# A condition for overfull experts, moved from between two stages to behind the last store

## The chip, the cores and the metric

The kernel runs on one core of a Trainium2 chip. The metric is device time of one execution in microseconds (us). The core has five engines that run side by side, each with an instruction queue of its own, and meet only through semaphores: TensorE (PE, with its weight loads shown apart as PEld), VectorE (DVE), ScalarE (ACT), GpSimd (POOL) and SyncE (SP), which issues most DMA transfers here. POOL issues the indirect ones, in which every row goes to an address of its own. A conditional jump is an instruction of an engine's sequencer. All five engines have to take the same decision, so each has its own copy of it.

## The reference

Three layers follow each other. The first is an attention in which a query sees only the keys whose six hash bits equal its own (2 batches, 8 heads, 768 positions, head size 64). Its output is 1536 tokens of 512 numbers. The second is a mixture of experts: each token goes to the one of 8 experts with the largest gate value.

```
e_idx = np.argmax(x @ w_gate, axis=1)
for e in range(E):
    mask = e_idx == e
    h = np.maximum(x[mask] @ w1[e], 0.0)
    out[mask] = gate_w[mask, None] * eom[mask, e, None] * (h @ w2[e])
```

The third is a feed-forward layer with a gated softmax (`solu = h * softmax(h)`), a normalization over 1024 channels, and a product with `w_out`.

```
h = x @ w_in
solu = h * softmax(h)
ln = (solu - mean(solu)) / sqrt(var(solu) + 1e-6) * g_ln
out = ln @ w_out
```

How many tokens an expert gets is known only on the chip. The draw used here gives the experts 192, 202, 210, 177, 218, 182, 193 and 162 tokens.

## The kernel before, in words

Every engine's instructions stand in the order in which the code writes them; there is no scheduler behind it. The Tile layer adds the semaphore waits.

The attention fills the first 250 us. It scatters each token's row, grouped by expert, to a table `xs` in memory, and counts the tokens of each expert. From the counts `totals` sorts the experts and works out where each one's columns start. It also computes a number `win[:, 3]`: how many extra passes ("windows" of `WIN = 160` tokens) are needed because an expert has more tokens than its capacity (`CAPS`: 224, 224, 224, 212, 200, 192, 184, 168 in sorted order, the first two being experts 0 and 1). For the counts above it is 0.

The expert stage runs 64 slots: four groups of `mm1` (L1167 to L1169) or `mm2` (L1196 to L1198) each. Every product is taken with fp16 high and low parts, so it has three matmuls. `ev2` evicts a result of `mm2` into `yT`, the transposed token columns: the high part by ACT (L1205), the low part by DVE (L1206, put off by one group through `run_late`). A column group of an expert starts at a position that is read from a register.

Behind the last slot stands `overflow()` (L1306; L1126 and L1127 are in it). Each engine loads `win[:, 3]` into a register and jumps over the body if it is 0. The body holds a loop over the extra windows with a full `mm1` and `mm2`.

The last stage (L1308 on) has 12 tiles of 128 tokens. `h2(t)` is 24 matmuls of 512 columns on PE (L1323) into a PSUM buffer of two banks, of which there are three. `solu_a` to `solu_d` are done by DVE, ACT and, for a power, POOL. The result is transposed by a DMA. `outp(t)` is 24 matmuls of 512 columns (L1391) and follows `h2(t + 4)` on PE. ACT evicts each output tile (L1395). For the last tile ACT takes the first 256 columns and DVE the other 256 (L1397). POOL copies the tile's row numbers to `tok` (L1399) and stores the tile with an indirect DMA (L1401). At the end of the program each engine drains, and all five meet at a barrier; those instructions carry L1452.

Some weights of the last stage (`w_in`, `w_out`) arrive as 64-bit floats. They are decoded piece by piece in free places of ACT (L125), POOL (L130, L152) and DVE (L135, L141, L146, L171).

Of the kernel before, what the change touches and what calls it, by code (L numbers as in the profile page):

```python
# [21 lines left out]
def kernel(  # L22
# [988 lines left out]
    with tc.manual_schedule():  # L1011
# [78 lines left out]

        wt["wo", 0] = yp.tile([128, 2, 4096], F16, name="wo")
        yT = yp.tile([128, 2, KD, NT + CAP], F16, name="yT")
        xw_t, hh_t = {}, {}

        def x_load(e, r0, w=CAP):
            xw = mp.tile([128, 2 * KD, CAP], F16, tag="xw", name="xw", bufs=3)
            x = nc.sync.dma_start_transpose(out=xw[:, :, 0:w], in_=xs[r0, :])
            xw_t[e] = xw
            if e in (1, "x"):
                for y in scattered:  # L1100
                    tc.add_manual_dep(x.ins, y.name, mybir.DependencyInfo(
                        mybir.DependencyClass.Sync, mybir.DependencyReason.DATA), reason="rows of xs")

        def window():

            d = nc.vector
            nf, sf, done = (exp_f[:, x] for x in range(3))
            f, win_f = (mp.tile([1, x, y], F32, tag=nm, name=nm, bufs=1) for x, y, nm in ((8, E, "wf"), (1, 3, "wg")))
            m = mp.tile([1, 1], F32, tag="wm", name="wm", bufs=1)
            d.tensor_tensor(out=f[:, 0], in0=nf, in1=done, op=ALU.is_gt)  # L1110
            d.scalar_tensor_tensor(out=f[:, 0], in0=iota8[0:1], scalar=1.0, in1=f[:, 0], op0=ALU.add, op1=ALU.mult)
            d.tensor_reduce(out=m, in_=f[:, 0], op=ALU.max, axis=AX.X)
            d.tensor_tensor(out=f[:, 0], in0=f[:, 0], in1=m.to_broadcast([1, E]), op=ALU.is_equal)
            d.tensor_scalar(out=f[:, 1], in0=nf, scalar1=-float(WIN), scalar2=None, op0=ALU.add)
            d.tensor_tensor(out=f[:, 1], in0=f[:, 1], in1=done, op=ALU.min)
            d.tensor_tensor(out=f[:, 2], in0=f[:, 1], in1=row0[0:1], op=ALU.add)
            d.tensor_tensor(out=f[:, 3], in0=f[:, 1], in1=sf, op=ALU.add)
            d.tensor_copy(out=f[:, 4], in_=iota8[0:1])
            d.tensor_tensor(out=f[:, 5:8], in0=f[:, 2:5], in1=f[:, 0:1].to_broadcast([1, 3, E]), op=ALU.mult)
            d.tensor_reduce(out=win_f[:, 0], in_=f[:, 5:8], op=ALU.add, axis=AX.X)  # L1120
            d.tensor_copy(out=win[:, 0:3], in_=win_f[:, 0])
            d.scalar_tensor_tensor(out=done, in0=f[:, 0], scalar=float(WIN), in1=done, op0=ALU.mult, op1=ALU.add)

        def overflow():
            why = "made on the chip from token counts"
            n = nc.values_load(win[:, 3:4], min_val=0, max_val=MW, skip_runtime_bounds_check_because=why)  # L1126
            with tc.If(n != 0), tc.For_i(0, n, 1) as i:  # L1127
                window()
                r0, c0, e0 = (
                    nc.values_load(win[0:1, x:x + 1], engines=g, min_val=0, max_val=mx,  # L1130
                                   skip_runtime_bounds_check_because=why)
                    for x, g, mx in ((0, [ET.SP], E * NT - WIN), (1, [ET.DVE, ET.Activation], NT), (2, [ET.SP], E - 1)))
                x_load("x", bass.ds(r0, WIN), WIN)
                for name, src, tag in (("w1", w1, "wa"), ("w2", w2, "wb")):
                    t16 = wp.tile([128, 2, 4096], F16, tag=tag, name=tag)
                    for c in range(4):
                        t = raw.tile([128, 1024], F32, tag="raw", name="raw")
                        if name == "w1":
                            nc.sync.dma_start(out=t, in_=src[bass.ds(e0, 1), c * 128:(c + 1) * 128, :]
                                              .rearrange("e p f -> (e p) f"))  # L1140
                        else:
                            nc.sync.dma_start(out=t.rearrange("p (f d) -> p f d", f=2),
                                              in_=src[bass.ds(e0, 1), c * 256:(c + 1) * 256, :]
                                              .rearrange("e (f p) d -> p (e f) d", p=128))
                        cs = slice(c * 1024, (c + 1) * 1024)
                        nc.scalar.activation(out=t16[:, 0, cs], in_=t, func=AF.Copy, scale=W_S)
                        nc.vector.scalar_tensor_tensor(out=t16[:, 1, cs], in0=t, scalar=W_S, in1=t16[:, 0, cs],
                                                       op0=ALU.mult, op1=ALU.subtract)
                    wt[name, "x"] = t16
                for g in range(4):  # L1150
                    ev1("x", g, mm1("x", g, WIN), WIN)
                    run_late()
                for g in range(4):
                    mm2("x", g, WIN)
                    ev2("x", g, c0, WIN)
                    run_late()
# [25 lines left out]
        def run_late():  # L1182
            for f in late:
                f()
            late.clear()
# [117 lines left out]
                nc.vector.tensor_scalar(out=csc, in0=mr[:, :, 0], scalar1=float(2.0 ** -22), scalar2=None,  # L1303
                                        op0=ALU.mult)
        run_late()
        overflow()  # L1306

        moe.close()  # L1308
        ps_a = ctx.enter_context(tc.tile_pool(name="ps_a", bufs=2, space=PSUM, reuse_waits="tile"))
        ps_h = ctx.enter_context(tc.tile_pool(name="ps_h", bufs=3, space=PSUM, reuse_waits="tile"))  # L1310
        mp = ctx.enter_context(tc.tile_pool(name="mq", bufs=2, reuse_waits="tile"))
# [73 lines left out]

        def outp(t):
            zT, fr = zT_t.pop(t), fr_t.pop(t)
            ps = ps_a.tile([128, DM], F32, tag="a", name="o")
            for f in range(KF):
                for a, w in ((0, 0), (0, 1), (1, 0)):  # L1390
                    nc.tensor.matmul(ps, zT[:, KF * a + f], w_o[:, w, f], start=(f == 0 and a == 0 and w == 0),  # L1391
                                     stop=(f == KF - 1 and a == 1))
            o = mp.tile([128, DM], F32, tag="o", name="o", bufs=3)
            na = DM if t < NTILE - 1 else DM // 2
            nc.scalar.activation(out=o[:, 0:na], in_=ps[:, 0:na], func=AF.Copy, scale=fr)  # L1395
            if na < DM:
                nc.vector.tensor_scalar(out=o[:, na:], in0=ps[:, na:], scalar1=fr, scalar2=None, op0=ALU.mult)  # L1397
            to = tok[:, t:t + 1]
            nc.gpsimd.tensor_scalar(out=to, in0=slot_f[:, t:t + 1], scalar1=1.0, scalar2=1.0, op0=ALU.mult,  # L1399
                                    op1=ALU.mult)  # L1400
            x = nc.gpsimd.indirect_dma_start(  # L1401
                out=out[:, :], out_offset=bass.IndirectOffsetOnAxis(ap=to, axis=0),
                in_=o, in_offset=None).ins
            for y in stored:
                tc.declare_no_dep(x, y, reason="every token has a row of its own")
            stored.append(x)
# [16 lines left out]
                outp(t - LAG)  # L1423
        for t in range(NTILE - 1 - LAG, NTILE):
            outp(t)


# [29 lines left out]
```

## Time and profile before

| | us |
|---|---|
| median of 3 runs | 526.81 (526.65 to 527.11) |
| profiled execution, its own time | 526.2 |
| its span, from the first to the last instruction | 524.4 |
| PE busy | 501.5 (96%) |
| DVE busy | 389.5 (74%) |
| ACT busy | 317.4 (61%) |
| POOL busy | 283.2 (54%) |

The profile is one execution. Its own time is 1.8 us above its span. All positions below are microseconds from the start of the span. A busy time says how long an engine had something in work. What an engine waited for stands in square brackets behind the instruction that ended the wait, or in the view of one source line. A letter q behind an engine (PEldq, POOLq, SPq) is its sequencer, where loads of registers, jumps, waits for semaphores and drains run. [...]

### The profile page before, as it was taken

The page shows a single profiled execution, that of the slowest core. Times are in us where ns is not written, and L with a number is a line of the kernel's source. Part 1 is how long each engine was busy: PE and PEld are TensorE (multiplying, and loading weights), DVE is VectorE, ACT ScalarE, POOL GpSimd, SP SyncE. Part 2 cuts the span into 40 slices and gives each one's busy share as a digit, 9 for nine tenths or more (in the row PEclk, how much of TensorE's full clock was granted, in tenths as well). Part 3 has the DMA queues.
Part 4 walks back from the last instruction along what each step waited for, and adds up shares of the span by engine and source line. Part 5 has one row for each costly group of instructions (what it writes and reads, how often), then busy time and mean ns, then how long its engine had stood idle before and what let it go on. Part 6 is the DMA issues. An engine that isn't in the chain of part 4 may idle for free. (4 is left out here: it accounts for less than half of the span.)

```text
span 524.4 us, 12447 instructions
## 1 busy us (share of the span) xinstructions
PE 501.5 (96%) x4692; PEld 384.7 (73%) x4692; DVE 389.5 (74%) x926; ACT 317.4 (61%) x595; POOL 283.2 (54%) x433
## 2 busy tenths in 40 slices
PE   7799999999999999997999999999979999999994
PEld 4578787888787888886999999999854444444442
DVE  7788888888888888766489898969934887455610
ACT  5778787888778887881364665566612455334420
POOL 7999896969879796826166587212111012212131
PEclk9999999999999999998999999999999999999998
DMA  5678988763837675302699999998500236352250
GB/s 180 144 201 188 243 151 236 194 184 86 201 115 126 200 174 167 78 2 81 194 288 227 314 307 296 272 313 279 173 5 0 55 76 112 80 96 66 61 140 40
DMA packets 107183, 83.23 MB, mean 159 GB/s; under 512 B 80624, under 2 KB 89456, under 8 KB 107120
## 3 DMA queue, kind: packets, MB, share of 16 engines
q1 hardware_dynamic: 104816, 76.09, 57.8%
q0 software_dynamic: 2304, 6.31, 3.1%
q8 instruction: 38, 0.62, 0.5%
q14 instruction: 25, 0.20, 0.1%
HBM read 51.43 MB, written 9.97 MB: 117 GB/s over the span
## 5 line engine op out<-in xcount | busy, mean ns | idle before, releaser
L627 PE MATMUL t<-ident,p 128*128 128x128 f32 x576 | 126.1, 275 | 0.5
L615 ACT ACTIVATE p<-s,mx 128x768 f32<-128x768 f32 x96 | 95.7, 997 | 38.7 <-DVE mx L604 22.4
L600 DVE TENSOR_REDUCE mx<-s 128x1 f32<-128x768 f32 x96 | 91.6, 955 | 27.0 <-PE s L590 21.6
L629 ACT COPY pt<-t 128x384 f32<-128x384 f32 x192 | 85.5, 479 | 7.0 <-PE t L627 5.8
L627 PEld LDWEIGHTS t<-ident,p 128*128 128x128 f32 x576 | 77.8, 141 | 15.4 <-ACT pt L629 8.9
L651 PE MATMUL v<-pt,v 128*64 128x128 f32 x1128 | 72.0, 277 | 0.0
L1323 PE MATMUL h<-wi,yT 128*128 128x512 f16 x288 | 65.2, 386 | 2.9 <-PEq L1127 2.9
L651 PEld LDWEIGHTS v<-pt,v 128*64 128x64 f32 x1128 | 60.6, 137 | 7.8 <-issue 6.8
L1197 PE MATMUL a<-hh,wb 128*128 128x224 f16 (+5 forms) x256 | 63.4, 251 | 2.0 <-DVE hh L1176 1.9
L1391 PE MATMUL o<-wo,zT 128*128 128x512 f16 x288 | 63.6, 379 | 0.1
L130 POOL TENSOR_SCALAR dm<-dm 128x512 f32<-128x512 f32 x16 | 33.2, 2072 | 56.4 <-ACT dm L125 56.2
L1196 PE MATMUL a<-hh,wb 128*128 128x224 f16 (+5 forms) x256 | 63.4, 251 | 0.0
L1198 PE MATMUL a<-hh,wb 128*128 128x224 f16 (+5 forms) x256 | 63.4, 251 | 0.0
L590 PE MATMUL s<-k,q 128*128 128x384 f16 x192 | 59.0, 329 | 1.0 <-ACT p L615 1.0
L590 PE MATMUL s<-b,cm 128*128 128x384 f16 x192 | 57.2, 326 | 1.4 <-DVE b L552 1.4
L1323 PEld LDWEIGHTS <-yT 128*128 128x128 f16 x288 | 28.6, 99 | 38.0 <-issue 5.4
L1167 PE MATMUL a<-xw,wa 128*128 128x224 f16 (+5 forms) x224 | 55.2, 249 | 0.3 <-DVE hh L1176 0.3
L1169 PE MATMUL a<-xw,wa 128*128 128x224 f16 (+5 forms) x224 | 55.2, 249 | 0.0
L1168 PE MATMUL a<-xw,wa 128*128 128x224 f16 (+5 forms) x224 | 55.2, 249 | 0.0
L1391 PEld LDWEIGHTS <-zT 128*128 128x128 f16 x288 | 28.2, 98 | 34.3 <-issue 0.4
L1401 POOL DMA_INDIRECT out_dram<-o,tok x12 | 12.6, 1047 | 53.8 <-issue 46.9
L1339 ACT ACTIVATE ex<-h,st,csc 128x1024 f32<-128x1024 f32 x12 | 14.4, 1203 | 41.8 <-DVE st L1362 27.6
(269 smaller groups left out, 1031.4 us busy)
## 6 DMA issues: line engine op xcount, KB each, us to landing
raw<-in_moe_w_dram SPq DMA_DIRECT2D x64, 512.0 KB, 6.1
raww<-in_moe_w_in_dram SPq DMA_DIRECT2D x8, 512.0 KB
raww<-in_moe_w_out_dram SPq DMA_DIRECT2D x8, 512.0 KB
xs<-raw SPq DMA_DIRECT2D x8, 448.0 KB, 4.0
v<-in_v_dram SPq DMA_DIRECT2D x8, 384.0 KB
q<-in_q_dram SPq DMA_DIRECT2D x6, 384.0 KB
k<-in_k_dram SPq DMA_DIRECT2D x6, 384.0 KB, 5.6
cm<-q SPq DMA_DIRECT2D x14, 96.0 KB, 2.1
```

The lines of the kernel that those rows point to most:

```text
L590: nc.tensor.matmul(t[:, c, 0:SB], d[x, h][:, s], flat(d[y, h])[:, c * SB:(c + 1) * SB], start=first, stop=not first)
L600: nc.vector.tensor_reduce(out=mx[:, 0:1], in_=t[:, :, 0:SB], op=ALU.max, axis=AX.XY)
L615: nc.scalar.activation(out=p, in_=s_t.pop(i)[:, :, 0:SB], func=AF.Exp, scale=mx[:, 1:2], bias=mx[:, 2:3], accum_out=sums[j][:, qt, h:h + 1])
L627: nc.tensor.transpose(t[:, g * 128:(g + 1) * 128], p[:, c, g * 128:(g + 1) * 128], ident)
L629: nc.scalar.copy(out=pt[i][:, 3 * c:3 * c + 3], in_=t[:, 0:SB].rearrange("p (g c) -> p g c", g=3))
L651: nc.tensor.matmul(o[64 * h:64 * h + 64], vt[:, h, c], ph[h][:, c], start=(c == 0), stop=(c == NS - 1), tile_position=(0, 64 * h))
L1167: nc.tensor.matmul(ps[:, i, 0:n], w[:, 0, kk, fs], xw[:, kk], start=(kk == 0), stop=False)
L1196: nc.tensor.matmul(ps, w[:, 0, f, ds], hh[:, 0, f], start=(f == 0), stop=False)
L1197: nc.tensor.matmul(ps, w[:, 0, f, ds], hh[:, 1, f], start=False, stop=False)
L1198: nc.tensor.matmul(ps, w[:, 1, f, ds], hh[:, 0, f], start=False, stop=(f == KF - 1))
L1323: nc.tensor.matmul(ps[:, c], yT[:, a, kk, ts], w_i[:, w, kk, c * 512:(c + 1) * 512], start=(kk == 0 and a == 0 and w == 0), stop=(kk == KD ...
L1391: nc.tensor.matmul(ps, zT[:, KF * a + f], w_o[:, w, f], start=(f == 0 and a == 0 and w == 0), stop=(f == KF - 1 and a == 1))
```

## The change

Four edits belong together.

1. `window()` and `overflow()` move behind the last `outp`. Nothing stands any more between the last slot of the expert stage and the last stage.
2. Since the last stage has then run without the extra tokens, the body of the condition runs the whole last stage once more after its loop. With a count of 0 the body is jumped over as before.
3. `yT` is set to zero before the expert stage, since columns of tokens over the capacity would otherwise be read before they are written.
4. The last output tile is computed in two halves of 256 columns, each with a PSUM buffer and 24 matmuls of its own, and both halves are evicted by ACT.

```
         yT = yp.tile([128, 2, KD, NT + CAP], F16, name="yT")
+        nc.gpsimd.memset(yT.bitcast(F32)[:, :, :, 0:NT // 2], 0.0)
...
         run_late()
-        overflow()
 
         moe.close()
...
         def outp(t):
             zT, fr = zT_t.pop(t), fr_t.pop(t)
-            ps = ps_a.tile([128, DM], F32, tag="a", name="o")
-            for f in range(KF):
-                for a, w in ((0, 0), (0, 1), (1, 0)):
-                    nc.tensor.matmul(ps, zT[:, KF * a + f], w_o[:, w, f], start=(f == 0 and a == 0 and w == 0),
-                                     stop=(f == KF - 1 and a == 1))
             o = mp.tile([128, DM], F32, tag="o", name="o", bufs=3)
             na = DM if t < NTILE - 1 else DM // 2
-            nc.scalar.activation(out=o[:, 0:na], in_=ps[:, 0:na], func=AF.Copy, scale=fr)
-            if na < DM:
-                nc.vector.tensor_scalar(out=o[:, na:], in0=ps[:, na:], scalar1=fr, scalar2=None, op0=ALU.mult)
+            for c0 in range(0, DM, na):
+                cs = slice(c0, c0 + na)
+                ps = ps_a.tile([128, DM], F32, tag="a", name="o")[:, 0:na]
+                for f in range(KF):
+                    for a, w in ((0, 0), (0, 1), (1, 0)):
+                        nc.tensor.matmul(ps, zT[:, KF * a + f], w_o[:, w, f, cs], start=(f == 0 and a == 0 and w == 0),
+                                         stop=(f == KF - 1 and a == 1))
+                nc.scalar.activation(out=o[:, cs], in_=ps, func=AF.Copy, scale=fr)
...
         for t in range(NTILE - 1 - LAG, NTILE):
             outp(t)
 
+        last.close()
+        stored.clear()
+        mp = ctx.enter_context(tc.tile_pool(name="mo", bufs=1, reuse_waits="tile"))
...
+        def overflow():
+            why = "made on the chip from token counts"
+            n = nc.values_load(win[:, 3:4], min_val=0, max_val=MW, skip_runtime_bounds_check_because=why)
+            with tc.If(n != 0):
+                with tc.For_i(0, n, 1):
+                    window()
...
+                for t in range(NTILE):
+                    solu_a(t, h2(t))
+                    solu_b(t)
+                    solu_c(t)
+                    solu_d(t)
+                    outp(t)
+
+        overflow()
```

In the order of the instructions the change shows at three places. The first is PE between the two stages. Before, the last `mm2` is followed by the load of the count, the jump, and the body of the condition:

```order
L1198 LDWEIGHTS wb
L1198 MATMUL a<-hh,wb 128x168
L1126 TENSOR_LOAD win [waits DVE_49]
L1127 COMPARE_AND_BRANCH x2
L1127 UNCONDITIONAL_BRANCH [waits PE_49]
L1127 UNCONDITIONAL_BRANCH [waits barrier_Pool_Activation_PE_DVE_SP_release]
L1452 BRANCH_PREFETCH_HINT
```

After the change `h2(0)` (now L1270) stands directly behind the last `mm2` (now L1145), with waits for the three engines that write what it reads:

```order
L1145 LDWEIGHTS wb
L1145 MATMUL a<-hh,wb 128x168
L1270 LDWEIGHTS yT [waits Activation_49,Pool_49]
L1270 MATMUL h<-wi,yT 128x512 [waits DVE_49]
L1270 LDWEIGHTS yT
L1270 MATMUL h<-wi,yT 128x512
```

The load and the jump are gone from here, and so are the rows of the body: on PE there are 385 rows from the `TENSOR_LOAD` to the first matmul weights of the last stage before. At the end of the program the jump now leads over some 1,590 rows on PE, 206 on DVE, 74 on ACT and 44 on POOL.

The second place is the end of ACT's queue, with the last output tiles. Before, one eviction of 256 columns ends it, and DVE does the other half:

```order
L1395 ACTIVATE o<-o,fr 128x512 [waits DMASW6_49,PE_49,Activation_49]
L1395 ACTIVATE o<-o,fr 128x512 [waits DMASW7_49,PE_49,Activation_49]
L1395 ACTIVATE o<-o,fr 128x256 [waits DVE_49,DMASW0_49,PE_49,Activation_49]
L1452 UNCONDITIONAL_BRANCH
```

Now ACT has both halves (L1344), and the load and the jump follow:

```order
L1344 ACTIVATE o<-o,fr 128x512 [waits DMASW7_49,PE_49,Activation_49]
L1344 ACTIVATE o<-o,fr 128x256 [waits DVE_49,DMASW0_49,PE_49,Activation_49]
L1344 ACTIVATE o<-o,fr 128x256 [waits PE_49]
L1400 TENSOR_LOAD win [waits DVE_49]
L1401 COMPARE_AND_BRANCH
```

The second half waits for PE alone. The third place is the end of POOL's queue. Before, the last store is followed by the end of the program:

```order
L1399 TENSOR_SCALAR tok<-slot_f 128x1
L1401 DMA out_dram<-o,tok 1536x512 [waits DMASW2_49,Activation_49,Pool_49]
L1399 TENSOR_SCALAR tok<-slot_f 128x1
L1401 DMA out_dram<-o,tok 1536x512 [waits DMASW3_49,DVE_49,Pool_49]
L1452 UNCONDITIONAL_BRANCH
L1452 ISA [waits barrier_Pool_Activation_PE_DVE_SP_gather]
```

After the change the path that jumps over the body ends the queue. It stands in the last three rows here; the two rows ahead of them are the end of the body, a store of the repeated stage:

```order
L1346 TENSOR_SCALAR tok<-slot_f 128x1
L1348 DMA out_dram<-o,tok 1536x512 [waits DMASW7_49,Activation_49,Pool_49]
L1401 UNCONDITIONAL_BRANCH
L1401 ISA [waits Pool_49,DMASW4_49,DMASW5_49,DMASW3_49,DMASW6_49,DMASW2_49,DMASW7_49,DMASW1_49,DMASW0_49]
L1401 UNCONDITIONAL_BRANCH
L1466 ISA [waits barrier_Pool_Activation_PE_DVE_SP_gather]
```

On this path POOL waits until all its stores have landed (DMASW0 to DMASW7), and then adds to their semaphores what the stores of the skipped body would have added (the `ISA` row of L1401). SP, which waits for these semaphores at the end of the program, goes on only then.

## Rows read from the trace of the kernel before

**Rows 1.** First part of the page: busy us (share of the span) xinstructions.

```profile
PE 501.5 (96%) x4692; PEld 384.7 (73%) x4692; DVE 389.5 (74%) x926; ACT 317.4 (61%) x595; POOL 283.2 (54%) x433
```

**Rows 2.** By stretch: length; PE, PEld, DVE, ACT, POOL busy; granted clock; DMA share, GB/s.

```profile
388.20:391.00 2.80, 0.00 (x0) 0.02 (x1) 0.51 (x1) 1.08 (x2) 1.08 (x1) 1.00 0.04 12
391.00:400.00 9.00, 8.99 (x34) 3.76 (x35) 2.50 (x4) 0.34 (x1) 0.84 (x1) 0.81 0.01 2
400.00:450.00 50.00, 50.00 (x233) 22.70 (x232) 36.95 (x99) 25.41 (x37) 8.67 (x13) 1.00 0.40 76
```

**Rows 3.** Timeline between the stages: start, us, instruction, [idle before, its releaser].

```profile
387.90 0.24 PE L1198 MATMUL a<-hh,wb 128*128 128x168 f16 x1
388.17 0.45 ACT L1205 ACTIVATE yT<-a 128x336 f32 x1 [3.03 <-PE a L1198]
388.65 0.51 DVE L1206 SCALAR_TENSOR_TENSOR yT<-a,yT 128x336 f32 x1 [2.97 <-ACT yT L1205]
391.01 2.60 PE L1323 MATMUL h<-wi,yT 128*128 128x512 f16 x7 [2.88 <-PEq L1127]
398.08 1.22 DVE L1336 TENSOR_REDUCE st<-h 128x1 f32<-128x1024 f32 x1 [5.05 <-PE h L1323]
```

**Rows 4.** L1126 and L1127 by sequencer: ns min/median/max, first and last start.

```profile
L1126 PEldq TENSOR_LOAD <-win x1: 486/486/486, 386.7 to 386.7; - x1
L1127 PEldq COMPARE_BRANCH  x1: 3423/3423/3423, 387.3 to 387.3; - x1
L1127 POOLq COMPARE_BRANCH  x1: 45/45/45, 374.7 to 374.7; - x1
```

**Rows 5.** Other gaps of PE, and the granted clock around them.

```profile
382.39 0.23 PE L1197 MATMUL a<-hh,wb 128*128 128x168 f16 x1 [0.95 <-DVE hh L1176]
380.00:384.00 4.00, 2.95 (x40) 2.67 (x38) 3.23 (x6) 0.32 (x1) 0.00 (x0) 1.00 0.02 4
240.00:244.00 4.00, 1.20 (x16) 0.94 (x17) 3.37 (x28) 0.30 (x1) 2.63 (x6) 1.00 0.18 70
244.00:248.00 4.00, 4.00 (x28) 3.41 (x26) 1.60 (x14) 0.00 (x0) 3.04 (x7) 0.60 0.34 138
392.00:394.00 2.00, 2.00 (x6) 0.76 (x5) 1.00 (x2) 0.00 (x0) 0.00 (x0) 0.50 0.00 0
```

**Rows 6.** Timeline of the last output tile, and one stretch of small matmuls.

```profile
517.56 0.47 ACT L1395 ACTIVATE o<-o,fr 128x256 f32<-128x256 f32 x1 [4.49 <-PE o L1391]
518.07 0.48 DVE L1397 TENSOR_SCALAR o<-o,fr 128x256 f32<-128x256 f32 x1 [15.38 <-ACT o L1395]
519.32 1.00 POOL L1401 DMA_INDIRECT out_dram<-o,tok  x1 [4.25 <-issue]
386.00:388.00 2.00, 2.00 (x30) 1.92 (x27) 0.00 (x0) 0.00 (x0) 0.00 (x0) 1.00 0.00 0
```

**Rows 7.** L1452 at the end of the program, by sequencer; and a small POOL instruction.

```profile
L1452 SPq EVENT_SEMAPHORE  x1: 17658/17658/17658, 504.4 to 504.4; - x1
L1452 SPq DRAIN  x2: 7/10/13, 522.6 to 522.7; - x2
L1452 POOLq DRAIN  x1: 4447/4447/4447, 519.1 to 519.1; - x1
514.88 0.19 POOL L1399 TENSOR_SCALAR tok<-slot_f 128x1 int32<-128x1 f32 x1
```

**Rows 8.** A memset, and POOL, DVE and PE at the start of the expert stage.

```profile
L305 POOL MEMSET raw<- x1: 942/942/942, 33.6 to 33.6; 128x1024 f32 x1
261.46 1.93 POOL L130 TENSOR_SCALAR dm<-dm 128x512 f32<-128x512 f32 x1 [11.05 <-ACT dm L125]
258.41 0.28 DVE L846 RECIPROCAL me<-rz 128x3 f32<-128x3 f32 x3
269.23 0.26 PE L1196 MATMUL a<-hh,wb 128*128 128x224 f16 x1
269.71 0.61 DVE L1176 SCALAR_TENSOR_TENSOR hh<-a,hh 128x448 f16<-128x448 f32 x1
```

More of the change, by code (lines that the diff above doesn't have):

```diff
@@ L1092 @@
         yT = yp.tile([128, 2, KD, NT + CAP], F16, name="yT")
+        nc.gpsimd.memset(yT.bitcast(F32)[:, :, :, 0:NT // 2], 0.0)
         xw_t, hh_t = {}, {}
         def x_load(e, r0, w=CAP):
-            xw = mp.tile([128, 2 * KD, CAP], F16, tag="xw", name="xw", bufs=3)
+            xw = mp.tile([128, 2 * KD, CAP], F16, tag="xw", name="xw", bufs=1 if e == "x" else 3)
             x = nc.sync.dma_start_transpose(out=xw[:, :, 0:w], in_=xs[r0, :])
@@ L1102, in x_load @@
                         mybir.DependencyClass.Sync, mybir.DependencyReason.DATA), reason="rows of xs")
[L1104 to L1156, printed above, removed]
@@ L1310 @@
         ps_h = ctx.enter_context(tc.tile_pool(name="ps_h", bufs=3, space=PSUM, reuse_waits="tile"))
-        mp = ctx.enter_context(tc.tile_pool(name="mq", bufs=2, reuse_waits="tile"))
+        last = ExitStack()
+        mp = last.enter_context(tc.tile_pool(name="mq", bufs=2, reuse_waits="tile"))
         w_i = wt["wi", 0].rearrange("p a (k f) -> p a k f", k=KD)
@@ L1425, with window @@
             outp(t)
+        last.close()
+        stored.clear()
+        mp = ctx.enter_context(tc.tile_pool(name="mo", bufs=1, reuse_waits="tile"))
+        def window():
+            d = nc.vector
+            nf, sf, done = (exp_f[:, x] for x in range(3))
+            f, win_f = (mp.tile([1, x, y], F32, tag=nm, name=nm, bufs=1) for x, y, nm in ((8, E, "wf"), (1, 3, "wg")))
+            m = mp.tile([1, 1], F32, tag="wm", name="wm", bufs=1)
+            d.tensor_tensor(out=f[:, 0], in0=nf, in1=done, op=ALU.is_gt)
+            d.scalar_tensor_tensor(out=f[:, 0], in0=iota8[0:1], scalar=1.0, in1=f[:, 0], op0=ALU.add, op1=ALU.mult)
+            d.tensor_reduce(out=m, in_=f[:, 0], op=ALU.max, axis=AX.X)
+            d.tensor_tensor(out=f[:, 0], in0=f[:, 0], in1=m.to_broadcast([1, E]), op=ALU.is_equal)
+            d.tensor_scalar(out=f[:, 1], in0=nf, scalar1=-float(WIN), scalar2=None, op0=ALU.add)
+            d.tensor_tensor(out=f[:, 1], in0=f[:, 1], in1=done, op=ALU.min)
+            d.tensor_tensor(out=f[:, 2], in0=f[:, 1], in1=row0[0:1], op=ALU.add)
+            d.tensor_tensor(out=f[:, 3], in0=f[:, 1], in1=sf, op=ALU.add)
+            d.tensor_copy(out=f[:, 4], in_=iota8[0:1])
+            d.tensor_tensor(out=f[:, 5:8], in0=f[:, 2:5], in1=f[:, 0:1].to_broadcast([1, 3, E]), op=ALU.mult)
+            d.tensor_reduce(out=win_f[:, 0], in_=f[:, 5:8], op=ALU.add, axis=AX.X)
+            d.tensor_copy(out=win[:, 0:3], in_=win_f[:, 0])
+            d.scalar_tensor_tensor(out=done, in0=f[:, 0], scalar=float(WIN), in1=done, op0=ALU.mult, op1=ALU.add)
@@ new lines, in overflow @@
+        def overflow():
[4 more added lines that the diff above has]
+                    window()
+                    r0, c0, e0 = (
+                        nc.values_load(win[0:1, x:x + 1], engines=g, min_val=0, max_val=mx,
+                                       skip_runtime_bounds_check_because=why)
+                        for x, g, mx in ((0, [ET.SP], E * NT - WIN), (1, [ET.DVE, ET.Activation], NT), (2, [ET.SP], E - 1)))
+                    x_load("x", bass.ds(r0, WIN), WIN)
+                    for name, src, tag in (("w1", w1, "wa"), ("w2", w2, "wb")):
+                        t16 = wp.tile([128, 2, 4096], F16, tag=tag, name=tag)
+                        for c in range(4):
+                            t = raw.tile([128, 1024], F32, tag="raw", name="raw")
+                            if name == "w1":
+                                nc.sync.dma_start(out=t, in_=src[bass.ds(e0, 1), c * 128:(c + 1) * 128, :]
+                                                  .rearrange("e p f -> (e p) f"))
+                            else:
+                                nc.sync.dma_start(out=t.rearrange("p (f d) -> p f d", f=2),
+                                                  in_=src[bass.ds(e0, 1), c * 256:(c + 1) * 256, :]
+                                                  .rearrange("e (f p) d -> p (e f) d", p=128))
+                            cs = slice(c * 1024, (c + 1) * 1024)
+                            nc.scalar.activation(out=t16[:, 0, cs], in_=t, func=AF.Copy, scale=W_S)
+                            nc.vector.scalar_tensor_tensor(out=t16[:, 1, cs], in0=t, scalar=W_S, in1=t16[:, 0, cs],
+                                                           op0=ALU.mult, op1=ALU.subtract)
+                        wt[name, "x"] = t16
+                    for g in range(4):
+                        ev1("x", g, mm1("x", g, WIN), WIN)
+                        run_late()
+                    for g in range(4):
+                        mm2("x", g, WIN)
+                        ev2("x", g, c0, WIN)
+                        run_late()
+                for t in range(NTILE):
[4 more added lines that the diff above has]
+                    outp(t)
```

## Prediction

> **What bounds the kernel now.** I read the parts of the page first, then busy time by stretch, then the timeline around the two places that the change touches, and last the views of the source lines that jump and that end the program. PE is in work for 96% of the span [rows 1], and in the last stage without a break: 50.00 us of 50 from 400 to 450 at the full clock [rows 2]. So in this stage whatever lets PE start earlier, or run faster, moves the end by as much. DVE has 36.95 us of work in the same stretch, ACT 25.41, POOL 8.67; none of them is near a bound.
>
> PE has one hole ahead of this stage: nothing at all from 388.20 to 391.00 [rows 2]. The timeline shows its edges [rows 3]. The last `mm2` matmul starts at 387.90 and lasts 0.24, so PE ends at 388.14. ACT evicts the high part until 388.62, DVE the low part until 389.16. PE starts `h2(0)` at 391.01, and the bracket names PE's own sequencer at L1127: the conditional jump. The views of these lines say the same [rows 4]: PE's sequencer loaded the count at 386.7, ahead of the array, began the jump at 387.3 and needed 3.42 us for it, until 390.7. POOL's copy of the jump took 0.045 us. So PE lost the time from 389.16, when its operands were there, to 391.01 to the jump alone.
>
> The hole has a second price. [...] DVE gets the first tile at 398.08 [rows 3], 7.07 us after PE began it, where 24 matmuls at the full clock take 24 x 0.2146 = 5.15 (50 us for 233, [rows 2]).
>
> **The change part by part.**
>
> *The hole.* The first matmul of `h2(0)` now waits for the last instruction of DVE's low part, so it can start when that ends, 389.16, plus the delay of a semaphore. For a matmul that waited for DVE the trace has one: 382.39 [rows 5]; I take 0.06. Start 389.22 instead of 391.01: -1.79. Nothing in front of ACT's or DVE's last eviction changes, so this wait stays as a hole of 1.08 us. It cannot be below 388.14, which would be -2.87, and a start 0.3 later would be -1.5.
>
> *The clock.* The trace has three gaps to judge by [rows 5]. After the 0.95 us gap ahead of 382.39 the clock stayed 1.00. From 240 to 244 PE was in work for 1.20 us only, and from 244 to 248 it got 0.60. The 2.88 us gap ahead of 391.01 was followed by 0.50. The hole that is left, 1.08 us, is next to the first of these, so I expect the clock to stay. That gives back (1 - 0.81) x 9.0 = 1.71 us. Ends: 0 and 1.92 (7.07 - 5.15).
>
> What is late next: PE and the engines behind it move forward together by 3.5 us, and the distance from `h2` to what frees its PSUM buffer stays what it was. The weight decode that runs into this stage no longer stands behind a jump.
>
> *The last tile.* 48 matmuls of 256 columns replace 24 of 512. Small matmuls run at nearly the same rate per column: 30 of 168 columns in 2.0 us [rows 6] are about 0.072 each with their overlap, 0.43 ns per column against 0.2146/512 = 0.42. I add 0.05. Before, after PE ended, ACT took 517.56 to 518.03 and only then DVE 518.07 to 518.55; POOL's store started 0.77 later [rows 6]. Now the first half is evicted while PE computes the second, and the store waits for one ACT instruction of the same shape as before (0.47): 518.03. That is -0.52, with the matmuls -0.47.
>
> *The memset.* 6144 fp32 numbers per partition. L305 needs 0.942 us for 1024 [rows 8], so 5.65 us. POOL is idle for the 11.05 us up to 261.46, that is from 250.41 [rows 8], and the memset waits for nothing later than the attention. It ends at about 256.1. What hides it is that idle time; without it POOL's decode at 261.46 would be late, and everything up to 5.65 us behind it. I count 0.
>
> *The tail.* Here the change adds waits, and no row shows one like them. Today SP's wait for the last store ends at 504.4 + 17.66 = 522.06, SP drains at 522.6, and POOL's drain lasts from 519.1 to 523.55 [rows 7]: POOL opens the final barrier, 1.49 us after the landing, and the span ends 0.85 later. After the change POOL loads the count and jumps while the store is under way, waits for the landing itself, adds to the semaphores, and only then can SP finish its waits (0.55 us) and POOL drain. Behind POOL's wait only its own drain is queued, but SP, and through the barrier all engines, wait for it. Bounds for the added instruction: 0.19 (a small POOL instruction, [rows 7]) and 1.00 (an indirect DMA on POOL, [rows 6]). If the drain then takes its 1.49 us anew, POOL is ready at 522.06 + 0.1 + (0.19 to 1.00) + 1.49 = 523.84 to 524.65, +0.3 to +1.1. If the drain's end was only the end of the store's own business, nothing is added. If a late drain is short, POOL and SP are ready at about 522.9, -0.6. I take +0.4, between the first two.
>
> The other jumps have cover. PE's can take its 3.42 us again, but its sequencer reached the jump 0.8 us before the array ended [rows 3, 4], so it is through 2.6 us after PE's last matmul, while today's end of POOL's drain comes 6 us after it. DVE and SP reach theirs before the last tiles.
>
> *Sum.* -1.79 - 1.71 - 0.47 + 0.4 = -3.57. Against the profiled execution's own 526.2 (524.4 and 1.8 around it) that is 522.6. The runs shown have a median of 526.81, 0.6 higher; the same saving gives 523.2, which I forecast, since the time will be a median of such runs.
>
> **The rivals.**
>
> *The clock falls all the same.* For it: PE was also short of work from 240 to 244 in pieces, and fell; a hole of 1.08 us lies above the 0.95 that did no harm. Against it: that stretch lacked 2.8 us of 4. Then only 1.79 + 0.47 - 0.4 = 1.86 is saved: 524.95.
>
> *The tail takes most of it.* A wait at the end replaces the one removed: if POOL's drain needs the time from the end of the store's issue (520.32) to 523.55, 3.2 us, after its last instruction of this kind, it ends at 522.06 + 0.1 + 1.0 + 3.2 = 526.4, +2.8. Saved is 3.97 - 2.8 = 1.2: 525.6. For it: the drain is the one long row of the end. Against it: it began before the store and may only reflect that.
>
> *POOL's jump becomes a long one.* A jump over PE's 385 rows took 3.42 us, one over POOL's short body 0.045 [rows 4]; POOL's body is longer now. At PE's price its jump would run from about 519.6 (519.1 and a load of 0.5, as PE's in [rows 4]) to 523.0, 1.0 past the landing: 524.2. For it: nothing shows from which length on a jump is long. Against it: POOL's 44 rows are far nearer to its short body than to PE's. [...]
>
> *It isn't the jump.* If PE's start at 391.01 were set by the handover of PSUM or by POOL, the jump being only the last thing seen, nothing but the last tile would change: -0.47 + 0.4, 526.7. Against it: all that PE waits for is done at 389.16.
>
> *Slower: the memset in the wrong place.* DVE sorts the experts just then, and finishes at 258.7 [rows 8]. Behind that chain stand the register loads of ACT and DVE and the first evictions. The fourth low part is done at 270.32, where PE, which starts `mm2` at 269.23 [rows 8], needs it some 18 matmuls later, at about 270.9: 0.6 us of slack. If the memset's writes held DVE up for its whole 5.65 us, PE would stand for 5.0 us and lose the clock once more (1.7): +6.7, so 529.9. It makes the kernel slower as soon as DVE is late by more than 3.5 us (0.6 + 3.57 + 1.05 - 1.7). Against it: DVE's instructions there are tiny, and a memset reads nothing.
>
> **How the numbers follow.** Forecast 0.69, the clock falls 0.12, the tail 0.06, POOL's jump 0.05, not the jump 0.04, the memset 0.04. The forecast's own range is 521.8 (from the profiled execution's level, the tail at -0.6 and the clock at 1.92 would give 521.4, of which I take most) to 524.2 (from the median's level, with a start 0.3 later and the tail at +1.1: -1.5 - 1.71 - 0.47 + 1.1 = -2.6). To hold 8 in 10 it must reach the case of the clock at 524.95 as well: 521.8 to 525.2. A measurement of this kernel can tell about 0.2%, 1.05 us, from no change. Faster is then the forecast, the cases of the clock and of POOL's jump, and half of the tail's, which lies on the edge: 0.69 + 0.12 + 0.05 + 0.03, less a little for the spread between runs, 0.88. Within 0.2%: the other half, and the jump's case, 0.08. Slower: 0.04.
>
> **What would show it.** Right: PE starts `h2(0)` about 1.1 us after the last `mm2`, released by DVE's low part of `yT`; the granted clock is 1.00 from there on; the first tile takes 5.2 us; behind PE's last matmul stands one ACT instruction of 0.47, then the store; POOL's memset lies between 250.4 and 256.2, and PE's first `mm2` still starts at about 269.2. Wrong: a start of `h2(0)` much after DVE's eviction, a clock under 1.00 behind it, a new hole at the first `mm2`, or more than 1.5 us added between the landing of the last store and the end.

## The result, and the profile after

The change made the kernel slower: 530.51 us (529.96 to 532.40, four runs) against 526.96 us for the kernel before beside it, a ratio of 1.0072 [1.0044, 1.0101], or 3.6 us between the medians. The forecast was 523.2.

The profiled execution took 532.4 us with a span of 530.5, 6.1 longer than the one of before. That is more than the 3.6 between the medians, since the profiled execution was the slowest of its four; the profile says where the time went, the medians how much it was. Cut at three marks (the first `mm1` matmul, the first `h2` matmul, the last store), the 6.1 fall into four parts:

| part of the span | before, us | after, us | difference |
|---|---|---|---|
| to the first `mm1` matmul (nothing changed there; 249.95 to 253.12 over the profiles of all kernels here) | 250.82 | 252.11 | +1.29 |
| expert stage, to the first `h2` matmul | 140.19 | 143.07 | +2.88 |
| last stage, to the last store | 128.31 | 126.11 | -2.20 |
| tail, from the store's start to the end | 5.08 | 9.21 | +4.13 |

The page first. PE's work is what it was (501.5 us, [rows 1]); its share fell because the span grew:

```profile
PE 501.6 (95%) x4716; PEld 387.3 (73%) x4716; DVE 392.3 (74%) x925; ACT 318.7 (60%) x596; POOL 289.6 (55%) x434
```

The timeline where the stages meet, as in [rows 3]:

```profile
393.86 0.24 PE L1145 MATMUL a<-hh,wb 128*128 128x168 f16 x1
...
394.61 0.51 DVE L1153 SCALAR_TENSOR_TENSOR yT<-a,yT 128x336 f32 x1 [2.97 <-ACT yT L1152]
395.18 1.02 PE L1270 MATMUL h<-wi,yT 128*128 128x512 f16 x4 [1.08 <-DVE yT L1153]
...
400.55 1.22 DVE L1283 TENSOR_REDUCE st<-h 128x1 f32<-128x1024 f32 x1 [2.23 <-PE h L1270]
```

The hole is 1.08 us and DVE releases it; the first tile reaches DVE 5.37 us after PE starts it, where [rows 3] had 7.07. By stretch, with the columns of [rows 2], where the granted clock is the share of TensorE's full clock that it got: the beginning of the expert stage, then the beginning of the last stage.

```profile
250.00:258.00 8.00, 3.89 (x41) 3.65 (x39) 4.78 (x10) 2.25 (x8) 6.94 (x4) 1.00 0.44 132
258.00:262.00 4.00, 4.00 (x25) 3.37 (x25) 3.59 (x25) 0.00 (x0) 0.00 (x0) 0.57 0.00 0
...
395.00:404.00 9.00, 8.82 (x41) 4.01 (x41) 3.13 (x9) 1.43 (x3) 1.92 (x1) 1.00 0.00 0
404.00:454.00 50.00, 50.00 (x233) 22.70 (x232) 37.82 (x99) 24.57 (x36) 8.71 (x14) 1.00 0.38 80
```

The clock that fell to 0.81 at the start of the last stage [rows 2] is 1.00 now. It falls in another place: 0.57 from 258 to 262. The kernel before, in one stretch over this place, was busy and at the full clock:

```profile
250.00:262.00 12.00, 11.29 (x120) 11.21 (x118) 6.45 (x54) 4.25 (x17) 0.94 (x2) 1.00 0.62 189
```

The timeline of after shows what stands there:

```profile
252.04 5.23 POOL L1093 MEMSET yT<- 128x6144 f32 x1
...
253.09 0.29 DVE L839 TENSOR_REDUCE rz<-rex 128x3 f32<-128x24 f32 x2 [5.84 <-ACT rex L833]
...
253.30 4.01 DVE L842 TENSOR_SCALAR rz<-rz 128x3 f32<-128x3 f32 x2
...
257.80 0.13 DVE L868 TENSOR_TENSOR tn<-m,row 128x8 f32<-128x8 f32 x1
...
257.98 0.26 PE L1114 MATMUL a<-raw,wa 128*128 128x224 f16 x1 [3.40 <-DVE tn L868]
```

POOL's memset ends at 257.27. Two DVE operations on three columns each, begun at 253.30, take 4.01 us together and end just behind it. The operations after them are short, but late. L868 reads the routing's PSUM tile `m`, and PE stands 3.40 us for it. The trace has 24 matmuls of `mm1`, one group, between 252.11 and this wait, so it is the second group that waits (the expectations below call it the fifth): its PSUM buffer takes the memory of `m`, which L868 frees.

The expert stage's +2.88 is made of several terms: +3.40 for the stand, (1 - 0.57) x 4.00 = +1.72 for the clock that fell behind it, -1.80 for the hole, and -0.4 because PE's waits for the DVE operations that write `hh`, the low part of `mm1`'s result, were 1.8 us in this execution and 2.2 in the one of before. These waits change from profile to profile: they are 2.2 to 6.3 us in the nine profiles without the stand, before among them, and 0.6, 1.8 and 4.5 in the three with it. So the length of this stage in one profile can't price a change.

The last tile, as in [rows 6]: ACT evicts the first half while PE computes the second.

```profile
517.48 0.47 ACT L1344 ACTIVATE o<-o,fr 128x256 f32<-128x256 f32 x1 [1.93 <-PE o L1342]
520.05 0.47 ACT L1344 ACTIVATE o<-o,fr 128x256 f32<-128x256 f32 x1 [2.10 <-PE o L1342]
521.29 1.00 POOL L1348 DMA_INDIRECT out_dram<-o,tok  x1 [3.74 <-issue]
```

The end, by line and sequencer as in [rows 4] and [rows 7]; L1401 is the condition, L1466 the end of the program, and INC_SWDGE_SEM is the row that stands there for the stores of the skipped body (run 4, without these stores, has none):

```profile
L1401 POOLq EVENT_SEMAPHORE  x5: 17/43/3244, 522.1 to 525.7; - x5
...
L1401 PEldq COMPARE_BRANCH  x1: 3422/3422/3422, 518.6 to 518.6; - x1
...
L1401 POOLq COMPARE_BRANCH  x1: 45/45/45, 521.6 to 521.6; - x1
...
L1401 POOLq INC_SWDGE_SEM  x1: 904/904/904, 525.8 to 525.8; - x1
...
L1466 POOLq DRAIN  x3: 40/107/3019, 526.7 to 530.3; - x3
```

The other engines' jumps take 0.045 to 0.072 us each, and PE's, 3.42 us long, is over at 522.0, before the store has landed. POOL, having jumped, waits for the store until 525.5, spends 0.90 us on INC_SWDGE_SEM, and only then begins a drain of 3.02 us, which ends 4.2 us after the landing. Before, the drain was queued right behind the store and ended 1.49 us after the landing [rows 7].

### The profile page after: what moved, and what is told of

It is laid out like the page before. It is cut to its first block, busy times and chain, and to the rows that moved or that the text cites. A ratio compares the mean times of both kernels' runs of the same rounds, so it can differ in the third digit from the quotient of the medians.

```text
span 530.5 us, 12494 instructions
## 1 busy us (share of the span) xinstructions
PE 501.6 (95%) x4716; PEld 387.3 (73%) x4716; DVE 392.3 (74%) x925; ACT 318.7 (60%) x596; POOL 289.6 (55%) x434
## 5 line engine op out<-in xcount | busy, mean ns | idle before, releaser
L1270 PE MATMUL h<-wi,yT 128*128 128x512 f16 x288 | 63.5, 379 | 1.1 <-DVE yT L1153 1.1
L1342 PE MATMUL o<-wo,zT 128*128 128x512 f16 (+1 forms) x312 | 63.7, 363 | 0.1
L1145 PE MATMUL a<-hh,wb 128*128 128x224 f16 (+5 forms) x256 | 63.4, 251 | 0.0
L1342 PEld LDWEIGHTS <-zT 128*128 128x128 f16 x312 | 30.5, 98 | 32.2 <-issue 0.4
L1270 PEld LDWEIGHTS <-yT 128*128 128x128 f16 x288 | 28.2, 98 | 35.0 <-issue 1.2
L167 ACT ACTIVATE wb<-raw 128x1024 f16<-128x1024 f32 x24 | 25.4, 1057 | 21.5 <-DMA raw<-in_moe_w_dram 21.4
```

Source lines behind the costliest of these rows:

```text
L1145: nc.tensor.matmul(ps, w[:, 1, f, ds], hh[:, 0, f], start=False, stop=(f == KF - 1))
L1270: nc.tensor.matmul(ps[:, c], yT[:, a, kk, ts], w_i[:, w, kk, c * 512:(c + 1) * 512], start=(kk == 0 and a == 0 and w == 0), stop=(kk == KD ...
L1342: nc.tensor.matmul(ps, zT[:, KF * a + f], w_o[:, w, f, cs], start=(f == 0 and a == 0 and w == 0), stop=(f == KF - 1 and a == 1))
```

## The experiments

All ratios are to the kernel before on the same chip. There its times spread from 525 to 534 us, so an effect under 0.3% is read from the profiles' marks, not from a ratio.

**1. Without the memset** (rows over capacity would then leave columns of `yT` unset).

```
-        nc.gpsimd.memset(yT.bitcast(F32)[:, :, :, 0:NT // 2], 0.0)
```

> The changed kernel without POOL's memset of `yT` (the columns of rows over capacity are then not set to zero ahead of the stage). Theory 1 (the memset holds one small DVE operation until it ends, so the PSUM buffer of the fifth `mm1` group is handed over late, PE stands 3.4 us and its clock falls for some 4 us): PE's 3.4 us before that group go, the granted clock stays 1.00 from 252 to 262 us, and the time falls by 3.4 + 1.7 = 5.1 us, to about 525.4 us, which is 1.5 us under the kernel before. Rival (the late start of the expert stage is chance or comes from elsewhere): the time stays at 530.5 us and the wait is there again.

Measured: 0.9995 [0.9974, 1.0016], median 528.74 against 529.17. PE's wait for L868 is gone, and 250 to 262 reads as before (11.29 us busy, clock 1.00). Against the 1.0072 of the changed kernel this is 0.77%, about 4.1 us: theory 1, a little smaller than expected. Half of the expectation fell: the kernel isn't 1.5 us faster than before but as fast, mostly because the memset was worth 4.1 us and not 5.1. The 4.1 is uncertain by about 2, as the two ratios come from different sets of runs, and a part of it may be tail: 8.03 us in this profile, 9.21 in the changed kernel's.

**2. The memset alone, on the kernel before.**

```
+        nc.gpsimd.memset(yT.bitcast(F32)[:, :, :, 0:NT // 2], 0.0)
```

> The kernel before, with POOL's memset of `yT` and nothing else of the change. Theory 1: about 5 us slower than before (532 us), with a DVE `rz` operation of some 4 us that ends with the memset and a PE wait of some 3.4 us before the fifth `mm1` group. Rival (the memset costs nothing by itself; what delays DVE is the new layout of memory or another part of the change): 527.0 us, no such wait.

Measured: 1.0049 [1.0027, 1.0071]. Its timeline and its waits of PE:

```profile
251.13 5.35 DVE L842 TENSOR_SCALAR rz<-rz 128x3 f32<-128x3 f32 x2
...
251.22 5.23 POOL L1093 MEMSET yT<- 128x6144 f32 x1
```

```profile
PE a L1168 <- DVE tn L868: 4.7, 1, 4.7
```

The same operations, the same wait, with nothing else of the change: the mechanism is the memset's. The time grew by 2.6 us, half of what was expected.

**3. The last tile in two halves alone.**

```
-            ps = ps_a.tile([128, DM], F32, tag="a", name="o")
...
+            for c0 in range(0, DM, na):
...
+                nc.scalar.activation(out=o[:, cs], in_=ps, func=AF.Copy, scale=fr)
```

> The kernel before, with the last output tile in two halves and nothing else of the change. As the prediction has it: 0.5 us faster (526.5 us), because only one 0.47 us copy of half a tile stands behind the last matmul instead of two in a row. Rival (the end is set by SP's and POOL's waits and drains, which the copy doesn't move): 527.0 us.

Measured: 1.0003 [0.9973, 1.0032], which can't tell 0.5 us from none. In its profile the last stage (first `h2` to last store) is 127.8 us where before had 128.3, with the old hole and the fallen clock: 0.5, as expected. The tail behind the earlier store is 5.10, as before, so the rival falls in this profile. The two numbers behind the changed kernel's -2.20 are then 0.5 from the halves and 1.7 from the clock.

**4. No memset, and no stores in the body's repeat.**

```
-        nc.gpsimd.memset(yT.bitcast(F32)[:, :, :, 0:NT // 2], 0.0)
...
-                    outp(t)
+                    outp(t, False)
```

> The changed kernel without the memset, and without the twelve stores of the repeated stage inside the body of the condition, which doesn't run here (the rest of the body stays). Theory 2 (the tail is long because POOL, on the path that skips the body, waits for the landing, writes the counter of its queue and drains, as the body holds stores of POOL's queue): from the last store's start to the end of the span about 5 us instead of 9.2, so 2.5 to 4 us under the run without the memset alone: 521.5 to 523 us. Rival (the tail is long because of the jumps over a long body): no difference to the run without the memset alone, 525.4 us.

Measured: 0.9937 [0.9905, 0.9969], 3.1 us under run 1 by the two ratios. POOL's wait, its INC_SWDGE_SEM and the drain behind it are gone. Run 1 first, then this run:

```profile
L1400 POOLq INC_SWDGE_SEM  x1: 904/904/904, 520.5 to 520.5; - x1
```

```profile
L1467 POOLq DRAIN  x3: 40/113/5772, 519.1 to 525.4; - x3
```

POOL's drain is queued behind the store again and ends 1.5 us after the landing. But the tail is 7.24 us in the profile, not 5, as the store lands late (4.9 us after its start): theory 2 holds for a part. The two profiles' tails differ by 0.8 us only; where the rest of the 3.1, which is uncertain by about 2, comes from is not shown.

**5. A short body between the stages.** The condition stays where it was before; inner loops shorten its body for PE; with the halves.

```
-                for g in range(4):
-                    ev1("x", g, mm1("x", g, WIN), WIN)
...
+                with tc.For_i(0, KF, 2) as f0:
...
+                with tc.For_i(0, KD, 2) as d0:
```

> The kernel before (condition between the two stages, no memset, no repeat), with the last tile in two halves and the condition's body written with inner loops over pairs of chunks, so that PE jumps over 144 matmuls and loads of weights instead of 384. Theory (PE's 3.42 us at the jump is paid for its length: DVE jumped over 247 instructions in 0.07 us): PE's COMPARE_BRANCH takes under 0.1 us, the hole ahead of the last stage is about 1.1 us instead of 2.9 to 3.1, the clock stays up, and the time falls by the 3.5 us of hole and clock, with the old tail of 5.1 us: 523 to 524 us where the kernel before has 527, 525.5 where it has 529. Rival (PE pays 3.4 us at any taken jump, or at a jump ahead of queued matmuls): no change beyond the halves, within 0.2% of before.

Measured: 0.9937 [0.9909, 0.9965], median 525.81 against 529.39. The jump, and PE's first `h2` matmul:

```profile
L1127 PEldq COMPARE_BRANCH  x1: 344/344/344, 390.9 to 390.9; - x1
```

```profile
392.82 0.38 PE L1343 MATMUL h<-wi,yT 128*128 128x512 f16 x1 [1.08 <-DVE yT L1226]
```

The jump takes 0.34 us, not under 0.1 as expected, but where 3.42 [rows 4] stood, 0.34 hides under the last `mm2` matmuls. The hole is 1.08, the last stage 126.1, the tail 5.06: the gains of the change without its costs. By the ratios it is faster than both kernels, and it keeps the handling of rows over capacity, which this input doesn't enter.

**6. The memset, without the operation that it holds.**

```
-                for t0, nt, l2, mx, df, ex, os_, z, osel, eo in w:
-                    d.tensor_scalar(out=z, in0=z, scalar1=1e-9, scalar2=None, op0=ALU.add)
```

> The changed kernel with the memset, without the DVE operation that adds 1e-9 to `rz` (the sum in the gate lacks that term). Theory 1a (what the memset holds is whatever DVE operation of a certain kind comes next; the next one has two SBUF inputs): the scalar_tensor_tensor on `rz` behind it is held instead for about 4 us, PE stands some 3.4 us before the fifth `mm1` group, and the time is that of the changed kernel. Rival 1b (only that one-input fp32 tensor_scalar is held): no DVE operation over 0.3 us there, no wait of PE over 0.6 us, 4 to 5 us faster than the changed kernel.

One profiled run, 530.53 us. DVE beside the memset (250.73 to 255.96):

```profile
250.73 5.23 POOL L1091 MEMSET yT<- 128x6144 f32 x1
...
252.32 0.28 DVE L842 SCALAR_TENSOR_TENSOR rz<-reo,rz 128x3 f32<-128x3 f32 x2
252.52 0.29 DVE L844 RECIPROCAL me<-rz 128x3 f32<-128x3 f32 x2
252.72 0.14 DVE L866 TENSOR_TENSOR tn<-m,row 128x8 f32<-128x8 f32 x1
...
254.28 0.21 DVE L877 TENSOR_REDUCE tso<-tgn 128x8 f32<-128x64 f16 x1
254.41 1.58 DVE L878 TENSOR_SCALAR tso<-tso 128x8 f32<-128x8 f32 x1
```

Fourteen groups of small operations (L839 to L877: reductions, a reciprocal, operations with two inputs) run through the memset at their usual length. The next one-input TENSOR_SCALAR is held until it ends (1.58 us). Rival 1b is right in kind, and PE's wait for the sort is gone. The gain of 4 to 5 us isn't there in the single time: the expert stage is 141.9 us (143.07 in after), with 4.7 us of waits for `hh`, and the tail is 9.60.

**7. The memset in 24 pieces.**

```
-        nc.gpsimd.memset(yT.bitcast(F32)[:, :, :, 0:NT // 2], 0.0)
...
+                    nc.gpsimd.memset(yz[:, za, zk, zc:zc + 256], 0.0)
```

> The changed kernel with the memset of `yT` as 24 pieces of 256 columns. Theory 1c (DVE is held until the POOL instruction that runs ends): each piece takes 5.23/24 = 0.22 us and a call's overhead, DVE gets in between two pieces, the held operation takes under 0.6 us, and PE's wait before the fifth `mm1` group is under 0.6 us: 4 to 5 us faster than the changed kernel. Rival 1d (DVE is held as long as POOL has one memset behind another): an operation of about 4 us or more, or each of the DVE operations there some tenths of a us longer, and a PE wait of 3 us or more.

One profiled run, 535.11 us:

```profile
250.41 6.14 POOL L1097 MEMSET yT<- 128x256 f32 x24
...
251.99 4.59 DVE L842 TENSOR_SCALAR rz<-rz 128x3 f32<-128x3 f32 x2
...
257.26 0.26 PE L1118 MATMUL a<-raw,wa 128*128 128x224 f16 x1 [3.99 <-DVE tn L868]
```

The pieces end at 256.55, the held operation at 256.58. The held operation doesn't get in between queued pieces: rival 1d.

**8. The condition at the end, short body, no repeat, no memset** (rows over capacity wouldn't reach the output).

```
-                for t in range(NTILE):
...
-                    outp(t)
```

> The changed kernel without the memset, with the condition behind the last store, but with neither the repeat of the last stage in its body nor PE's long jump (the body of the short form, rows over capacity would not reach the output). Theory 2a (the condition behind the last store costs its 2 to 4 us of tail by the long jump's code and the body's POOL work): from the last store's start to the span's end 5.1 to 5.6 us, and the time 2.5 us or more under the run without the memset alone. Rival 2b (any condition behind the last store delays the landing or POOL's drain): 7.2 us as without the body's stores, or more.

Measured: 0.9952 [0.9918, 0.9986]; the tail is 5.59 us. That is theory 2a for the tail. The time is 2.3 us under run 1's by the two ratios, where 2.5 or more was expected. A condition behind the last store costs 0.5 us here, and nothing in run 10, if its body has no repeat.

**9. The whole change, with the two held operations in a form with two inputs.**

```
-                    d.tensor_scalar(out=z, in0=z, scalar1=1e-9, scalar2=None, op0=ALU.add)
+                    d.scalar_tensor_tensor(out=z, in0=z, scalar=1e-9, in1=z, op0=ALU.add, op1=ALU.max)
...
+            d.scalar_tensor_tensor(out=so[:, 1], in0=so[:, 0], scalar=float(NT), in1=so[:, 0], op0=ALU.mult, op1=ALU.max)
```

> The whole changed kernel, memset included, with the two small one-input fp32 operations that the memset was seen to hold (the 1e-9 on `rz`, the product by 1536 on `tso`) written with the same tile as a second input, same result. Theory 1b (a one-input fp32 tensor_scalar or a copy is held by POOL's memset, one with two inputs isn't): both take 0.2 to 0.4 us, at most a cast or copy behind them is held; PE's 3.4 us before the fifth `mm1` group are gone, and the time is that of the run without the memset, 0.3% below the kernel before to 0.2% above it. Rival (the time lost to the memset is given back later anyway, since PE waits for DVE's and the DMAs' decoded weights further on): the wait is gone, but the time stays at that of the changed kernel, 0.5 to 1% above before.

Measured: 1.0007 [0.9976, 1.0038], where the change had 1.0072 [1.0044, 1.0101]. DVE beside a memset that ends at 256.90:

```profile
253.24 0.28 DVE L842 SCALAR_TENSOR_TENSOR rz<-rz 128x3 f32<-128x3 f32 x2
...
255.59 0.16 DVE L880 SCALAR_TENSOR_TENSOR tso<-tso 128x8 f32<-128x8 f32 x1
255.78 1.15 DVE L881 CAST slot_i<-tso 1x24 int32<-1x24 f32 x1
255.87 1.06 DVE L883 TENSOR_TENSOR tg<-to,cw__89 1x64 f16<-1x64 f16 x1
256.05 0.90 DVE L885 COPY exp_f<-tn 1x8 f32<-1x8 f32 x1
```

The same memset, and no wait of PE for L868. The cast is held now, which no matmul waits for at once. The operations queued behind it (L883, which has two inputs, and the copies) end with it or just after, so these rows can't tell whether a copy would be held by itself. That is theory 1b: by the two ratios about 3.4 us come back from two small changes, uncertain by about 2. The rival asked for 0.5 to 1% above before and falls. The profile alone wouldn't show the gain: its expert stage is 143.7 us where after had 143.07, since PE waits 6.3 us for `hh` in it.

**10. As run 8, with the body of the kernel before.**

```
-                for t in range(NTILE):
...
-                    outp(t)
```

> As the end condition with the short body, no memset and no repeat, but with the body of the kernel before, so that PE jumps far (384 matmuls and loads of weights) while POOL has no work of its own in the body (rows over capacity would not reach the output). Theory 2c (PE's long jump, whose code is fetched while the last store is under way, makes the 7.2 us of tail that were left without the body's stores): PE's COMPARE_BRANCH 3.4 to 3.7 us, the tail from the store's start about 7 us, the time 1.5 us or more over the short form's. Rival 2d (it is POOL's own work in the body, whose counters it must raise on the path that skips it): the tail stays at 5.1 to 5.7 us, the same time as the short form's.

Measured: 0.9901 [0.9864, 0.9937], seven runs. Its condition, and the end of its program:

```profile
L1400 PEldq COMPARE_BRANCH  x1: 450/450/450, 517.2 to 517.2; - x1
```

```profile
L1459 POOLq DRAIN  x3: 45/113/3712, 520.3 to 524.6; - x3
```

The tail is 5.08 us. The premise failed: PE's jump over the same body that took 3.42 us between the stages takes 0.45 here. So the run doesn't tell 2c from 2d; it shows again that a condition behind the last store, without the repeat in its body, leaves the tail as it was.

The tails side by side, one profile each (us; the landing is the end of the sequencer's wait for the last store, SP's or, with the full repeat, POOL's):

| kernel | store to landing | landing to the end of POOL's drain | tail |
|---|---|---|---|
| before; halves alone (run 3); short body (run 5) | 2.7; 2.7; 2.7 | 1.5; 1.5; 1.5 | 5.1; 5.1; 5.1 |
| at the end, no repeat (runs 8, 10) | 3.2; 2.7 | 1.5; 1.5 | 5.6; 5.1 |
| repeat without stores (run 4) | 4.9 | 1.5 | 7.2 |
| full repeat: after; runs 1, 6, 7, 9 | 4.2; 3.1; 4.6; 4.2; 4.9 | 4.2; 4.2; 4.2; 4.2; 4.2 | 9.2; 8.0; 9.6; 9.2; 9.9 |

The late landing has a trace of its own. The end of before (from 511.4, two stores) and of after (from 517.5), by DMA queue (packets, MB, share) and by time to landing:

```profile
q0 software_dynamic: 160, 0.52, 1.4%
out_dram<-o,tok POOLq DMA_INDIRECT x2, 2.7
```

```profile
q0 software_dynamic: 160, 0.52, 1.6%
q8 instruction: 2, 0.03, 0.2%
q14 instruction: 3, 0.02, 0.1%
out_dram<-o,tok POOLq DMA_INDIRECT x1, 4.2
```

One store is 80 packets of q0. In the five profiles where it lands after 2.7 us (before, runs 2, 3, 5, 10) all of them are through 2.4 us after its start, and no packet of the queues marked as instruction moves beside them. In the other seven 2 to 8 of the 80 come later, the last 2.6 to 4.4 us after the start, and one to three instruction packets move beside them. Run 4 is one of the seven, without a POOL store in its body. So the late landing and these packets come together; no run changed the packets alone, so the cause is not shown.

## Why the prediction was wrong

**The hole: right.** 2.88 became 1.08 us, released by DVE's low part; -1.79 forecast, -1.80 found. Run 5 gets the same hole without moving the condition.

**The clock: right.** -1.71 forecast, (1 - 0.81) x 9.0 us of [rows 2]; the last stage shrank by 2.20, of which the halves are 0.5 (run 3). The granted clock stayed at 1.00 behind the hole of 1.08 us, so the rival of a clock that falls all the same was wrong.

**The last tile: right**, -0.47 forecast, 0.5 found.

**The memset: the first step that failed.** The text says "What hides it is that idle time" and "I count 0". It looked at what POOL had to do, and for DVE at a price it called unlikely since "DVE's instructions there are tiny, and a memset reads nothing". Being tiny didn't help: three columns were held for 4.01 us. The rival with this mechanism was placed wrong. It put PE's stand at the first `mm2` at 269; PE stood ahead of the second `mm1` group, until 258, for L868, in the middle of the chain that was held. It also took L846, a step of the gates, for the end of the sort; in before the sort is through with L897 at 256.97. Its 5.0 us of standing and 1.7 of clock were 3.40 and 1.72, together 5.1, in the profile. That its 529.9 lies near the measured 530.5 is luck: it had the tail at +0.4. In the times the memset is worth 4.1 us (run 1), 3.4 (run 9) and 2.6 (run 2). Why the times show less than 5.1 stays open. Some may come back, as PE waits less for `hh` later in the stage, but these waits spread as widely (2.2 to 6.3 us without the stand, 0.6 to 4.5 with it) as what they would have to explain.

What the prediction didn't weigh is the kind of DVE's operations, and the traces of the runs tell them apart by it. Beside the memset the one-input TENSOR_SCALARs took 4.01 us (after) and 1.58 (run 6), and the cast 1.15 (run 9). The reductions, the reciprocal and the two-input operations that weren't queued behind a held one were not held: in run 6 they took 0.14 to 0.29 us for one or two of them, and in run 9 the operations of those two lines took 0.28 and 0.16 in a two-input form. In run 7 DVE was held for 4.59 us, to the end of the last of 24 queued memsets. Why the kind matters no run shows.

**The tail: the second step that failed.** "I take +0.4" measured +4.13 in the profile. The step offered three readings of POOL's drain (+0.3 to +1.1, nothing, -0.6) and took a value between the first two; none was long enough. The rival that read it as 3.2 us of its own after POOL's last instruction, +2.8 in all, had it nearly right: 0.90 and 3.02, the same to the digit in each of the five profiles with the full repeat. With the waits between them the drain ends 4.2 us after the landing instead of 1.5: +2.7. Run 4 shows that the stores in the body make this part. The other 0.3 to 2.2 is a landing that comes later, a term that the sum didn't have at all. The place of the condition alone doesn't make it (0 in run 10, 0.5 in run 8), nor do the stores in the body (2.2 in run 4). Whether POOL's other work in the body delays it, or what the queues marked as instruction move beside the store, stays open: in run 10 both were gone. Packets of these queues, one to three, moved beside the store in all seven profiles in which some of its own came late.

**POOL's jump: the rival fell**, 0.045 us over the long body as over the short one.

So the gains were there, -1.80 and -2.20. Against them stood 2.6 to 4.1 us for the memset (runs 2, 9 and 1) and 3.0 to 4.8 for the tail (the five profiles): +1.6 to +4.9 in all, with the 3.6 measured between.

## What to carry to other kernels

Before giving an idle engine a long instruction, list what its neighbour does in that stretch by kind of operation (here a memset of 5.23 us held TENSOR_SCALARs on three columns for 4.01), and follow the first thing that waits for that chain, down to the PSUM buffer that it frees. Look at what stands in the body that a condition skips: here stores of POOL's queue in it cost 2.7 us more after the last landing even though they never ran. Where a jump makes the hole, try a shorter jump (run 5: 0.34 us where 3.42 stood) before moving it.

## What the runs showed of the hardware that was not expected

- A memset on POOL of 5.23 us held one-input TENSOR_SCALAR (4.01 us in after) and CAST (1.15 us in run 9) of DVE until it ended, and queued memsets held a TENSOR_SCALAR without a break (4.59 us over pieces of 0.26 in run 7). The 4.01 us are the operations' own time, with no wait for a semaphore ahead of them, so the section on the chip is too narrow where it has the engines meet only through semaphores.
- PE's taken jump over the same 384 matmuls and loads of weights costs 3.42 to 3.64 us between the stages (before, runs 2 and 3) and 0.45 at the end of the program (run 10); over 144 it costs 0.34 (run 5) and 0.45 (run 8); with the repeat in the body 3.33 to 3.73. Length alone doesn't set the price, and what does was not tried further.
- POOL's drain behind INC_SWDGE_SEM takes 3.02 us (all five profiles with it), where one that was queued before the landing ends 1.5 us after it.
